# One half of a weight matrix loaded by sixteen DMAs of eight partitions, in a decode-attention kernel

## The chip, the cores and the metric

The kernel runs on one core of a Trainium2 chip. The metric is device time in microseconds (us): the median of three runs of the kernel before is 692.73 us (691.97 to 692.79). Beside these runs there is one profiled execution, which has its own time and from which all durations below are taken.

## The reference, cut to what matters

Two sequences of one token each attend to a cache of 32,768 positions, with 32 query heads on 8 key/value heads of 128 elements. The attention output goes through `wo`, and a small MLP on the same normalized token gates it.

```python
xn = layernorm(A_x)                                  # [2, 1, 512]
q  = (xn @ wq)                                       # 32 heads of 128
o  = softmax(q . k_cache / sqrt(128)) @ v_cache      # caches: [2, 8, 32768, 128] bf16 each
s  = o.reshape(2, 1, 4096) @ wo                      # wo: [4096, 512] bf16
g  = silu(xn + gelu(layernorm(xn) @ w3) @ w4)        # on one token the shifted branch is zero
out = x + s * g
```

The two caches are 268 MB together; every byte of them is read once. `wo` is 4.2 MB.

## The kernel before, in words

The work is cut into 16 units, one for each pair of a sequence and a key/value head (`units`, line 57), and each unit into four chunks of 64 blocks of 128 positions (`NCH` is 4). A chunk of K or of V is one load of 2 MB into one of eight buffers of the pool `slots` ([128 partitions, 8192] bf16; lines 62 and 99). The list `loads` (lines 85 to 92) fixes the order: the first K chunk, `wq` in two loads, the other K chunks of unit 0, `w3`, `w4`, and then K of the next unit and V of this unit in turn. The main loop (lines 376 to 390) walks this list, works on entry i and then issues the load of entry i + 8, into the buffer that entry i has just left. A partition of such a load is one run of 16 KB in memory.

All loads are issued by SyncE (SP) in this order, and SP waits in order too. A load waits for two things: for TensorE to have read the buffer's last content (a semaphore of PE), and for the semaphore that it will raise itself. There are eight of these for DMAs, taken in turn (DMAHW0 to DMAHW7 in the built program), so a DMA waits until the eighth DMA before it has landed.

A K chunk (`k_job`, line 263) is transposed on TensorE, eight blocks at a time (line 250), copied out of PSUM by VectorE or ScalarE in the ratio two to one (lines 253 and 255), and multiplied with the four queries of the unit (line 204). `softmax_front` takes the unit's maximum and the exponentials (line 239). A V chunk (`v_job`, line 275) is multiplied with the probabilities (line 282). `unit_end` (line 296) puts four partial sums together (line 306) and, after every second unit, multiplies four heads with their rows of `wo` (line 316).

`wo` lies in a buffer of its own, `wo_sb` with [128, 32, 512] (line 83). Row h * 128 + p of the matrix goes to partition p, head h. It is loaded in two halves of 16 heads, 2 MB each: the first after the last K chunk of unit 1 (line 388), the second after the first K chunk of unit 2 (line 390). A partition of a half is 16 runs of 1 KB. The first half is needed first by line 316 of unit 1.

Of the kernel before, what the change touches and what calls it, by code (L numbers as in the profile page):

```python
# [22 lines left out]
def kernel(  # L23
# [14 lines left out]
    nc = tc.nc  # L38
# [4 lines left out]
    Hq = HD // Dh  # L43
# [35 lines left out]
    wo_v = A_wo.rearrange("(h p) d -> p h d", p=128)  # L79
# [3 lines left out]
    wo_sb = pers.tile([128, Hq, D], BF16)  # L83
# [11 lines left out]
    def issue(i):  # L95
        if i >= len(loads):
            return
        what = loads[i]
        t = slots.tile([128, UT * Dh], BF16, tag="slot", name=f"slot_{what[0]}")
        if what[0] in ("K", "V"):  # L100
            b, g = units[what[1]]
            c = what[2]
            src = A_k_cache if what[0] == "K" else A_v_cache
            nc.sync.dma_start(
                out=t[:, :],
                in_=src[b, g, c * CH:(c + 1) * CH, :].rearrange("(p t) d -> p (t d)", p=128),
            )
        elif what[0] == "wq":
            k0 = what[1] * 2
            nc.sync.dma_start(  # L110
                out=t[:, 0:2 * HD].rearrange("p (k f) -> p k f", k=2), in_=wq_v[:, k0:k0 + 2, :])
        elif what[0] == "w3":
            nc.sync.dma_start(
                out=t[:, 0:DK * Fdim].rearrange("p (k f) -> p k f", k=DK), in_=w3_v)
        else:
            nc.sync.dma_start(
                out=t[:, 0:FK * D].rearrange("p (f d) -> p f d", f=FK), in_=w4_v)
        tiles[what] = t
# [51 lines left out]
    for j, src in enumerate((xn_bf, ln2_bf)):  # L170
        sv = src[:, :].rearrange("b (p k) -> b k p", k=DK)
        for k in range(DK):
            nc.tensor.transpose(
                out=treg[:, (j * DK + k) * B:(j * DK + k + 1) * B],
                in_=sv[:, k, :], identity=ident[0:B, 0:B])
# [87 lines left out]
    def k_job(n, c):  # L263
        kv = tiles[("K", n, c)][:, :].rearrange("p (t d) -> p t d", d=Dh)
        for blk in range(NB):
            transposed(n, c, blk, kv)
            if n == 0 and c == 0 and blk < KTB - 1:
                if blk == KTB - 2:
                    q_job()
                continue  # L270
            flush(LAG)
            if glue and blk >= 2:
                glue.pop(0)()

    def v_job(n, c):
        vv = tiles[("V", n, c)]
        pr = unit_st[n]["p"]
        for i in range(UT // 16):
            for j in range(4):
                v0 = i * 16 + j * 4  # L280
                u0 = c * UT + v0
                nc.tensor.matmul(  # L282
                    acc[32 * j:32 * j + 16, :],
                    lhsT=pr[:, u0:u0 + 4, :].rearrange("p u h -> p (u h)"),
                    rhs=vv[:, v0 * Dh:(v0 + 4) * Dh],
                    start=(c == 0 and i == 0), stop=(c == NCH - 1 and i == UT // 16 - 1),
                    tile_position=(0, 32 * j),
                )
            if i == 0:
                flush(0)  # L290
        if c == NCH - 1:
            unit_end(n)
# [83 lines left out]
    for i, what in enumerate(loads):  # L376
        if what[0] == "K":
            k_job(what[1], what[2])
        elif what[0] == "V":
            if what[2] == 0:  # L380
                while glue and "p" not in unit_st[what[1]]:
                    glue.pop(0)()
            v_job(what[1], what[2])
        elif what == ("w4",):
            mlp_job()
        issue(i + SLOTS)
        if what == ("K", 1, NCH - 1):
            nc.sync.dma_start(out=wo_sb[:, 0:Hq // 2, :], in_=wo_v[:, 0:Hq // 2, :])
        if what == ("K", 2, 0):
            nc.sync.dma_start(out=wo_sb[:, Hq // 2:Hq, :], in_=wo_v[:, Hq // 2:Hq, :])  # L390
    while glue:
# [37 lines left out]
```

## Time and profile before

| what | value |
|---|---|
| median of three runs | 692.73 us |
| the profiled execution, its own time | 692.67 us |
| its span (first to last instruction) | 690.9 us |
| TensorE busy (matmul) | 557.7 us, 81% of the span |
| VectorE busy, ScalarE busy | 294.1 us and 244.9 us |
| read from memory | 280.50 MB, 406 GB/s over the span |
| mean granted TensorE clock | 0.83 of full speed |

The profile shows one execution. Its second part cuts the span into 40 slices and gives the busy share of each engine in tenths, and below that the mean busy share of the core's 16 DMA engines and what they moved. The third part counts the DMA packets by queue: one is a run of data or a small write that raises a semaphore. The fourth follows the chain of work that ended last back from the end. Views by stretch of time give the same shares for any stretch, the timeline gives single instructions, and the list of waits gives who waited for whom. The trace also keeps, for each DMA, the moments at which the engines that carried it raise its semaphore, and the start, length, size and queue of every packet, but not which engine carried it.

### The profile page before, as it was taken

How to read it: one execution, taken by the hardware profiler on the slowest of the kernel's cores; microseconds unless marked ns; L12 is line 12 of the kernel's file. 1: busy time of each engine (PE TensorE's matmuls, PEld its weight loads, DVE VectorE, ACT ScalarE, POOL GpSimd, SP SyncE). 2: the span in 40 equal slices, each digit the busy share in tenths (PEclk: the TensorE clock that was granted, in tenths of full speed). 3: DMA queues.
4: the chain of work that ended last, by engine and by line, in shares of the span. 5: the costliest groups of instructions: out<-in, count | busy, mean ns of one | idle time of the engine just before them, and what ended most of it. 6: DMA issues, size and time to landing. Idle time of an engine off the chain costs nothing.

```text
span 690.9 us, 20959 instructions
## 1 busy us (share of the span) xinstructions
PE 557.7 (81%) x9662; PEld 468.2 (68%) x9662; DVE 294.1 (43%) x548; ACT 244.9 (35%) x370; POOL 0.9 (0%) x7
## 2 busy tenths in 40 slices
PE   3888998596887988989787869879778896979755
PEld 2885877475876767777676757767676675868633
DVE  4253544232544443534443534344444353445321
ACT  1245343142432433343343424224343342434220
POOL 0000000000000000000000000000000000000000
PEclk9696989678898795868998987799999798799875
DMA  8999999999999999999999999999999999999960
GB/s 360 426 424 427 422 424 401 394 431 421 426 424 423 429 424 424 423 424 426 425 425 426 420 424 428 425 425 424 421 425 428 425 422 426 425 424 426 424 281 18
DMA packets 23231, 281.83 MB, mean 408 GB/s; under 512 B 2148, under 2 KB 6248, under 8 KB 6248
## 3 DMA queue, kind: packets, MB, share of 16 engines
q1 hardware_dynamic: 23144, 280.51, 96.5%
q8 instruction: 75, 1.23, 0.7%
q14 instruction: 12, 0.10, 0.0%
HBM read 280.50 MB, written 0.00 MB: 406 GB/s over the span
## 4 chain that ended last, share of the span: by engine, by line
DMA 63%; PE 30%; ACT 3%; DVE 2%; issue 1%; SPq 0%; ACTq 0%; DVEq 0%
DMA slot_K<-in_A_k_cache_dram 55%; PE tT L250 16%; DMA slot_V<-in_A_v_cache_dram 5%; PE sc L204 4%; PE ot L306 3%; DMA slot_wq<-in_A_wq_dram 2%; PE s_ps L316 2%; ACT ktb L253 2%; PE acc L282 2%; ACT pr L239 1%; PE bc L233 1%; PE ot L304 1%; PE h L363 1%; DVE ktb L255 1%; PE qT L329 1%
## 5 line engine op out<-in xcount | busy, mean ns | idle before, releaser
L250 PE MATMUL tT<-ident,slot_K 128*128 128x128 bf16 x4096 | 349.5, 244 | 80.8 <-DMA slot_K<-in_A_k_cache_dram 78.6
L250 PEld LDWEIGHTS <-slot_K 128*128 128x128 bf16 x4096 | 284.0, 111 | 115.6 <-DMA slot_K<-in_A_k_cache_dram 100.2
L255 DVE COPY ktb<-tT 128x1024 bf16<-128x1024 bf16 x342 | 230.8, 691 | 239.3 <-PE tT L250 238.4
L253 ACT COPY ktb<-tT 128x1024 bf16<-128x1024 bf16 x170 | 172.4, 1014 | 329.1 <-PE tT L250 328.9
L204 PE MATMUL sc<-q_sb,ktb 128*128 128x4 bf16 x4096 | 179.1, 166 | 14.9 <-ACT ktb L253 13.6
L204 PEld LDWEIGHTS <-ktb 128*128 128x128 bf16 x4096 | 155.6, 99 | 43.9 <-ACT ktb L253 26.0
L282 PE MATMUL acc<-slot_V,pr 128*16 128x512 bf16 x1024 | 84.7, 414 | 15.7 <-DMA slot_V<-in_A_v_cache_dram 11.9
L213 DVE TENSOR_REDUCE pm<-sc 128x4 f32<-128x256 f32 x64 | 27.2, 426 | 83.8 <-ACT scS L212 83.8
L239 ACT ACTIVATE pr<-scS,nb 128x256 bf16<-128x256 f32 x64 | 45.0, 853 | 15.8 <-DVE nb L235 15.8
L212 ACT COPY scS<-sc 128x256 f32<-128x256 f32 x64 | 23.8, 372 | 61.9 <-PE sc L204 61.9
L282 PEld LDWEIGHTS <-pr 128*16 128x16 bf16 x1024 | 20.7, 89 | 30.2 <-issue 17.4
L306 PE MATMUL ot<-sel,acs 128*128 128x4 f32 x128 | 23.1, 303 | 0.0
L306 PEld LDWEIGHTS ot<-sel,acs 128*128 128x128 f32 x128 | 22.4, 262 | 0.0
L300 DVE COPY acs<-acc 128x512 f32<-128x512 f32 x16 | 10.9, 683 | 19.1 <-PE ot L306 18.7
L239 ACT ACTIVATION_READ_ACCUMULATOR pr<-scS,nb 128x1 f32 x64 | 16.3, 254 | 0.0
L316 PE MATMUL s_ps<-wo_sb,oT_sb 128*2 128x512 bf16 x32 | 13.2, 559 | 0.5 <-DVE oT_sb L311 0.5
L310 DVE RECIPROCAL rc<-ot 128x4 f32<-128x4 f32 x16 | 2.9, 182 | 23.2 <-PE ot L306 23.2
L233 PE MATMUL bc<-dg,ones_f 4*128 4x4 f32 x32 | 7.5, 301 | 1.3 <-DVE dg L228 1.3
L304 PE MATMUL ot<-S,ones_f 128*128 128x4 f32 x32 | 7.5, 305 | 1.1 <-DVE oT_sb L311 1.1
L329 PE MATMUL qT<-xT,slot_wq 128*128 128x2 bf16 x128 | 3.7, 165 | 5.1 <-DMA slot_wq<-in_A_wq_dram 5.1
L304 PEld LDWEIGHTS ot<-S,ones_f 128*128 128x128 f32 x32 | 6.4, 250 | 2.0 <-DVE oT_sb L311 1.2
L233 PEld LDWEIGHTS bc<-dg,ones_f 4*128 4x128 f32 x32 | 6.1, 237 | 2.1 <-DVE dg L228 1.3
(58 smaller groups left out, 60.2 us busy)
## 6 DMA issues: line engine op xcount, KB each, us to landing
slot_K<-in_A_k_cache_dram SPq DMA_DIRECT2D x64, 2048.0 KB, 31.7
slot_V<-in_A_v_cache_dram SPq DMA_DIRECT2D x64, 2048.0 KB, 35.1
slot_wq<-in_A_wq_dram SPq DMA_DIRECT2D x2, 2048.0 KB, 14.7
wo_sb<-in_A_wo_dram SPq DMA_DIRECT2D x2, 2048.0 KB, 21.0
slot_w<-in_B_w_dram SPq DMA_DIRECT2D x2, 1792.0 KB
x_bf<-in_A_x_dram SPq DMA_DIRECT2D x1, 2.0 KB
out_dram<-out_bf SPq DMA_DIRECT2D x1, 2.0 KB
```

Source lines behind the costliest of these rows:

```text
L204: nc.tensor.matmul(sc[:, u * rep:(u + 1) * rep], lhsT=ktb[:, i, :], rhs=q_sb[:, b, g * rep:(g + 1) * rep], start=True, stop=True,)
L212: nc.scalar.copy(out=st["scS"][:, :, c * UT:(c + 1) * UT], in_=scv)
L213: nc.vector.tensor_reduce(out=st["pm"][:, :, c], in_=scv, axis=AX.X, op=ALU.max)
L233: nc.tensor.matmul(bc[:, :], lhsT=ones_f[0:rep, :], rhs=st["dg"][:, :], start=True, stop=True)
L239: nc.scalar.activation(out=pr[:, :, h], in_=st["scS"][:, h, :], func=ACT.Exp, bias=nb[:, h:h + 1], scale=inv_sqrt_dh, accum_out=S4[:, h:h ...
L250: nc.tensor.transpose(out=tT[:, i, :], in_=kv[:, blk * TB + i, :], identity=ident[:, :])
L253: nc.scalar.copy(out=ktb[:, :, :], in_=tT[:, :, :])
L255: nc.vector.tensor_copy(out=ktb[:, :, :], in_=tT[:, :, :])
L282: nc.tensor.matmul(acc[32 * j:32 * j + 16, :], lhsT=pr[:, u0:u0 + 4, :].rearrange("p u h -> p (u h)"), rhs=vv[:, v0 * Dh:(v0 + 4) * Dh], s ...
L304: nc.tensor.matmul(ot[:, rep:2 * rep], lhsT=ones_f[:, :], rhs=st["S4"][:, :], start=True, stop=True)
L306: nc.tensor.matmul(ot[:, 0:rep], lhsT=acs[:, i * Dh:(i + 1) * Dh], rhs=sel[:, i, :], start=(i == 0), stop=(i == 3))
L316: nc.tensor.matmul(s_ps[:, :], lhsT=oT_sb[:, h, :], rhs=wo_sb[:, h, :], start=(h == 0), stop=(h == Hq - 1))
```

## The change

Only the load of the first half of `wo` is changed. The 128 partitions are taken in 16 groups of eight: group (q, i) has the partitions 32q + i, 32q + i + 4, and so on to 32q + i + 28. Each group is a DMA of [8 partitions, 16 heads, 512], 128 KB in 128 runs of 1 KB. The same bytes go to the same places. The other half, and every other load, is as before.

```diff
         issue(i + SLOTS)
         if what == ("K", 1, NCH - 1):
-            nc.sync.dma_start(out=wo_sb[:, 0:Hq // 2, :], in_=wo_v[:, 0:Hq // 2, :])
+
+            wo_8 = A_wo.rearrange("(h q j i) d -> q i j h d", q=4, j=8, i=4)
+            for q in range(4):
+                for i in range(4):
+                    p0 = 32 * q + i
+                    nc.sync.dma_start(
+                        out=wo_sb[p0:p0 + 29:4, 0:Hq // 2, :], in_=wo_8[q, i, :, 0:Hq // 2, :])
         if what == ("K", 2, 0):
             nc.sync.dma_start(out=wo_sb[:, Hq // 2:Hq, :], in_=wo_v[:, Hq // 2:Hq, :])
```

The built program of the changed kernel has the same instructions in the same order on TensorE, VectorE, ScalarE and GpSimd. On SP the one DMA of line 388 is replaced by sixteen of line 393, between the same two neighbours. Each of the sixteen waits for the next of the eight DMA semaphores, as every DMA here does; the V load behind them waits for DMAHW0, which the ninth of the sixteen raises.

## The prediction

> **What bounds the kernel now.** I read the page's slices first: are the DMA engines ever free?
>
> ```profile
> span 690.9 us, 20959 instructions
> DMA  8999999999999999999999999999999999999960
> GB/s 360 426 424 427 422 424 401 394 431 421 426 424 423 429 424 424 423 424 426 425 425 426 420 424 428 425 425 424 421 425 428 425 422 426 425 424 426 424 281 18
> DMA packets 23231, 281.83 MB, mean 408 GB/s; under 512 B 2148, under 2 KB 6248, under 8 KB 6248
> q8 instruction: 75, 1.23, 0.7%
> DMA 63%; PE 30%; ACT 3%; DVE 2%; issue 1%; SPq 0%; ACTq 0%; DVEq 0%
> ```
>
> They are full from start to near the end, and 63% of the chain that ended last is transfers. The dip to 401 and 394 GB/s is where `wo` is loaded. Then I read the end in stretches of time (columns: stretch, length, busy time of PE, PEld, DVE, ACT, POOL, clock, DMA share, GB/s):
>
> ```profile
> 648.00:652.00 4.00, 1.98 (x41) 1.02 (x37) 0.49 (x2) 1.38 (x2) 0.00 (x0) 1.00 1.03 438
> 660.00:664.00 4.00, 1.70 (x23) 0.79 (x23) 1.76 (x6) 1.24 (x4) 0.00 (x0) 0.86 0.69 291
> 668.00:672.00 4.00, 1.72 (x16) 0.44 (x9) 0.00 (x0) 0.00 (x0) 0.00 (x0) 0.79 0.48 205
> 676.00:680.00 4.00, 2.37 (x19) 0.97 (x18) 0.00 (x0) 0.00 (x0) 0.00 (x0) 0.50 0.01 4
> ```
>
> At 668 us half of the sixteen engines have nothing left. The semaphore events of the last V load say the same: eight engines end at 661.4 to 667.0 us, the other eight at 675.0 to 677.6. In the first K load all were within 1.2 us. What parts them is instruction loads: 75 packets of 16 KB on q8, of about 1.1 us. Followed by their start times, they take eight engines in turn, and each visit sets an engine back 1.5 us. So **there are eight late engines, which fetch instructions, and eight early ones**, and the end (677.6, and 13.3 us of last V product, sums and output) hangs on the late eight alone.
>
> Last, SP's timeline where `wo` is issued:
>
> ```profile
> 89.20 0.33 SPq L104 DMA_DIRECT2D slot_K<-in_A_k_cache_dram  x1
> 89.58 0.43 SPq L388 DMA_DIRECT2D wo_sb<-in_A_wo_dram  x1
> 91.11 27.58 SPq L104 DMA_DIRECT2D slot_V<-in_A_v_cache_dram  x1
> 118.78 0.73 SPq L104 DMA_DIRECT2D slot_K<-in_A_k_cache_dram  x1
> ```
>
> The V load behind `wo` was issued for 27.58 us: its descriptors went in only when `wo` began to drain. This costs nothing, because the engines had earlier loads to do. The events give, for that place: the K load issued at 89.20 lands on the early engines at 114.6 to 116.0 and on the late ones at 116.3 to 119.0; `wo` 5.9 us later on each (120.5 to 121.9, and 122.2 to 124.9); V 4.9 us after that.
>
> **The change, part by part.**
>
> *Which engines carry the sixteen DMAs.* The packets under 512 B are semaphore writes: 134 loads over 128 partitions at 16 each are 2144, and 4 are left for the two DMAs of two partitions (x_bf and the output), two each. So a DMA of two partitions runs on two engines, and I take it that one of eight runs on eight. [...]
>
> *Bytes per engine.* A half of `wo` costs an engine 5.9 us (114.62 to 120.53 on the first, 119.02 to 124.85 on the last). On eight engines it is twice that, 11.8 us, or 0.74 us for each of the sixteen. So eight engines get +5.9 us and eight get -5.9 us, and all hangs on whether the loaded eight are the late ones.
>
> *Issue and waits.* Fifteen more issues at 0.33 to 0.43 us are 5 to 6.5 us of SP, which is no cost in itself: SP sat 27.58 us in this place. But each waits for the eighth DMA before it, and that binds here as elsewhere:
>
> ```profile
> SPq L104 <- DMA slot_K<-in_A_k_cache_dram: 55.2, 31, 3.8
> ```
>
> DMAs 1 to 7 of the sixteen wait for loads landing up to 113.9 and go out in time. The eighth waits for the K load that lands at 119.0. The ninth waits for the first of the sixteen, and the V load behind them for the ninth. Until then nothing is queued for the other eight engines: they run dry from 116 to 119 us on.
>
> *If the early eight carry the load.* The ninth lands at 116.0 + 9 x 0.74 = 122.7. SP also needs nine issues (eighth to sixteenth) from 119.0 on at a step of 0.40 to 0.47 us (x_bf to K at the start, and the issues of 136 to 138 us), so V is issued at 122.7 to 123.25. From issue to first packet the first K load took 0.97 us on its first engine and 1.83 on its last, so the late engines start V at 123.7 to 125.1, where before the last of them started at 124.85. They skip 5.9 us of `wo` and stand idle for nearly all of it: -1.2 to +0.2, and I take **-0.6 us**, nearer the first rows because a step of 0.40 is what a short row of issues showed when nothing was queued. The early eight end at 661.4 to 667.0 plus 5.9, at most 672.9, still ahead.
>
> *The second half and the next V.* V issued behind the second half was held 14.76 us (120.08) without an engine going dry. Now the loaded eight reach that half at 116.0 + 11.8 + 2 x 4.9 = 137.6, which releases that V; the others need it at 124.4 + 2 x 4.9 + 5.9 = 140.1. About 1.5 us of cover is left after the 0.97; if it is gone, each us late is a us on the end.
>
> *Consumers.* Line 316 reads the first half from 143.9 us on. It would land at 127.8 or 130.8 instead of 124.9, still 13 us early. No engine but SP has another instruction. At 134.9 TensorE waits for a K load, which moves by some us; it is made up, since TensorE is 81% busy and does not set the end.
>
> [...]
>
> **The rivals.**
>
> A, the forecast: the loaded eight are the early ones. 692.67 - 0.6 = **692.1 us**, own range 691.4 to 693.0. The profiled time stands 0.06 below the median, so nothing is added.
>
> B, slower: the fetching engines are among the loaded eight. Then the last of them does all sixteen from 119.0 to 130.8 instead of 124.9; V waits for the ninth only until 125.7 and is there in time, so there is no further gap. 677.6 + 5.9, and 692.67 + 5.9 = **698.6** (697.5 to 699.3; less, 695.6, if only a fetching engine that ends 2.6 us earlier is loaded). It decides as soon as one of the three engines that end last is loaded. [...]
>
> C, nothing is shifted: the DMAs are spread over sixteen engines, by shape or by partition. Bytes per engine stay. The sixteenth is issued at 122.3 to 122.8, the queue is just short, and V starts at about 125.0 to 125.3 instead of 124.9: **692.9**.
>
> D, as A but no gap, if the waits hold less than I read: the early eight end last, at 672.9, 4.7 us before 677.6: **688.0**. The list of waits speaks against it.
>
> **How the numbers follow.** A 0.52, B 0.36, C 0.07, D 0.05. What a measurement of this kernel can tell from no change is about 0.2%, 1.4 us. Of A, 0.14 may end beyond it on the faster side (a gap shorter than reckoned), 0.02 on the slower. Faster: 0.14 + 0.05 = 0.19. Slower: 0.36 + 0.02 + 0.02 of C = 0.40. Same: 0.41. The range goes from A's lower end to B's upper, 691.2 to 699.2, because B alone is more than 2 in 10.
>
> **What would show it.** Packets: with eight engines each, 16 x 8 - 16 = 112 more (23343, and 2260 under 512 B); with sixteen, 240 more. Semaphore events: the sixteen land about 0.74 us apart. A stretch of some 4 to 5 us with a DMA share near 0.5 around 119 to 124. At the end, A has the early engines finish at 667 to 673 us and the late ones still at 677, so the stretch at half share shrinks to a few us; B has both some 6 us later (early ones idle from 116 to 126.7, late ones at 683), and the stretch keeps its length. I am wrong at the root if the sixteen run on all engines, or if the V load behind them is issued before 121 us.

## The result, and the profile after

The changed kernel takes **697.69 us** (median of four runs, 697.12 to 698.46) against 692.42 of the kernel before on the same chip (691.97 to 692.79): ratio 1.0077, 95% interval 1.006 to 1.0095. It is 5.3 us slower. The profiled execution took 698.25 us.

The page after, the lines that answer to those shown of before:

```profile
span 696.5 us, 20977 instructions
DMA  8999998899999999999999999999999999999970
GB/s 361 426 422 429 421 425 331 309 407 420 428 423 425 426 423 424 424 426 424 423 426 423 424 428 423 426 423 427 421 425 427 422 427 423 424 425 423 426 322 22
DMA packets 23343, 281.83 MB, mean 405 GB/s; under 512 B 2260, under 2 KB 6360, under 8 KB 6360
q8 instruction: 75, 1.23, 0.7%
DMA 68%; PE 26%; ACT 2%; DVE 1%; SPq 1%; issue 1%; ACTq 0%; DVEq 0%
```

The packets have grown by 112: each of the sixteen runs on eight engines. Slices 7 and 8 (104 to 139 us) fell from 401 and 394 to 331 and 309 GB/s. Slice 9 fell from 431 to 407, since the second half of `wo` now lands in it (144.6 to 146.5 us). All others up to the end are within 8 GB/s of what they were, so the time was lost in this one place and not made up. SP's timeline there:

```profile
88.52 0.33 SPq L104 DMA_DIRECT2D slot_K<-in_A_k_cache_dram  x1
88.90 36.70 SPq L393 DMA_DIRECT2D wo_sb<-in_A_wo_dram  x16
125.71 0.40 SPq L104 DMA_DIRECT2D slot_V<-in_A_v_cache_dram  x1
126.21 0.37 SPq L104 DMA_DIRECT2D slot_K<-in_A_k_cache_dram  x1
```

In the kernel before, the V load was handed to its queue from 91.1 us on; now SP comes to it at 125.71. Stretches of time around that, and at the end (stretch, length, busy PE, PEld, DVE, ACT, POOL, clock, DMA share, GB/s):

```profile
118.00:120.00 2.00, 0.81 (x12) 0.82 (x13) 0.11 (x1) 0.00 (x0) 0.00 (x0) 0.91 0.42 149
124.00:126.00 2.00, 1.60 (x42) 1.56 (x40) 1.34 (x2) 1.03 (x2) 0.00 (x0) 1.00 0.47 138
128.00:130.00 2.00, 0.00 (x0) 0.00 (x0) 0.00 (x0) 0.00 (x0) 0.00 (x0) 0.97 1.11 245
...
668.00:672.00 4.00, 1.51 (x16) 0.54 (x17) 0.00 (x0) 2.43 (x8) 0.00 (x0) 0.50 0.81 336
676.00:680.00 4.00, 1.74 (x16) 0.54 (x16) 0.00 (x0) 0.00 (x0) 0.00 (x0) 0.50 0.47 201
680.00:684.00 4.00, 0.99 (x16) 0.31 (x15) 0.00 (x0) 0.00 (x0) 0.00 (x0) 0.50 0.14 57
```

At 118 to 126 us about half of the engines or fewer have work (a share of 0.42 to 0.52). At 128 us all are busy and still move only 245 GB/s, which is something else than idleness. At the end the stretch at half share lies some 6 us later than before (205 GB/s at 668 to 672 us then; 201 at 676 to 680 now).

The semaphore events give the same by load. The K load ahead of the sixteen lands at 114.6 to 119.1 us, as before. The first of the sixteen lands on six of its engines at 115.4 to 116.3 and on two at 118.7 and 118.8: **six of the loaded engines are early ones and two are late ones**. The sixteenth lands at 128.7 to 131.0. The V load behind lands at 133.8 to 135.7 on all sixteen (125.5 to 129.8 before): the lead that the early engines had is used up, and the last engine is 5.9 us later. The last V load of the kernel ends at 669.5 to 675.8 on the early engines and at 680.1 to 683.1 on the late ones, 5.5 us later than before at its end.

### The profile page after: what moved, and what is told of

Its sections match the earlier page's. It is cut to its first block, busy times and chain, and to the rows that moved or that the text cites. A ratio compares the mean times of both kernels' runs of the same rounds, so it can differ in the third digit from the quotient of the medians.

```text
span 696.5 us, 20977 instructions
## 1 busy us (share of the span) xinstructions
PE 551.3 (79%) x9662; PEld 463.0 (66%) x9662; DVE 293.8 (42%) x548; ACT 244.7 (35%) x370; POOL 0.9 (0%) x7
## 4 chain that ended last, share of the span: by engine, by line
DMA 68%; PE 26%; ACT 2%; DVE 1%; SPq 1%; issue 1%; ACTq 0%; DVEq 0%
DMA slot_K<-in_A_k_cache_dram 60%; PE tT L250 14%; DMA slot_V<-in_A_v_cache_dram 5%; PE sc L204 3%; DMA slot_wq<-in_A_wq_dram 2%; PE ot L306 2%; PE s_ps L316 2%; ACT ktb L253 1%; PE acc L282 1%; SPq L393 1%; ACT pr L239 1%; PE h L363 1%; PE bc L233 1%; PE ot L304 1%; PE qT L329 1%
## 5 line engine op out<-in xcount | busy, mean ns | idle before, releaser
L306 PE MATMUL ot<-sel,acs 128*128 128x4 f32 x128 | 20.6, 284 | 0.0
L306 PEld LDWEIGHTS ot<-sel,acs 128*128 128x128 f32 x128 | 19.8, 236 | 0.0
L316 PE MATMUL s_ps<-wo_sb,oT_sb 128*2 128x512 bf16 x32 | 11.4, 494 | 0.5 <-DVE oT_sb L311 0.5
L329 PEld LDWEIGHTS <-slot_wq 128*128 128x128 bf16 x128 | 3.5, 104 | 5.5 <-DMA slot_wq<-in_A_wq_dram 5.5
```

The source lines that it names most:

```text
L306: nc.tensor.matmul(ot[:, 0:rep], lhsT=acs[:, i * Dh:(i + 1) * Dh], rhs=sel[:, i, :], start=(i == 0), stop=(i == 3))
L316: nc.tensor.matmul(s_ps[:, :], lhsT=oT_sb[:, h, :], rhs=wo_sb[:, h, :], start=(h == 0), stop=(h == Hq - 1))
L329: nc.tensor.matmul(qT_ps[:, h * B:(h + 1) * B], lhsT=w[:, (k % 2) * HD + h * Dh:(k % 2) * HD + (h + 1) * Dh], rhs=xT[:, k, :], start=(k == ...
```

## The experiments

Three explanations were kept apart. *Shift*: two of the eight loaded engines are late ones, and carry twice their share of half a `wo`. *Gap*: the V load is held behind the sixteen, and the engines run dry. *Write side*, which came up after the second run: the time depends on which partitions the eight engines write.

| run | us, median | ratio to before, 95% interval |
|---|---|---|
| the change | 697.69 | 1.0060 to 1.0095 |
| e1 sixteen DMAs, one head each, 128 partitions | 694.54 | 1.0024 to 1.0049 |
| e2 the sixteen, one behind each of the first 16 loads | 707.04 | 1.0200 to 1.0229 |
| e3 the sixteen carry one head, one DMA the rest | 700.75 | 1.0105 to 1.0136 |
| e4 small probes in the kernel before | 692.77 | one run |
| e5 as e2, into partitions 0 to 63 only | 695.86 | 1.0044 to 1.0068 |
| e6 as e2, upper partitions first | 706.84 | 1.0182 to 1.0215 |
| e7 small probes in the changed kernel | 698.60 | one run |
| e8 half of the last V load over 125 partitions | 695.75 | 1.0041 to 1.0070 |
| e9 eight consecutive partitions each | 705.01 | 1.0159 to 1.0205 |
| e10 the change, into partitions 0 to 63 only | 696.42 | 1.0045 to 1.0075 |
| e11 the sixteen on ScalarE's queue | 708.40 | 1.0212 to 1.0246 |
| e12 as e11, into partitions 0 to 63 only | 707.65 | 1.0211 to 1.0242 |
| e13 one cache load cut into DMAs of 25, 25, 5, 5, 4 and 64 partitions | 702.01 | 1.0129 to 1.0159 |
| e14 two such loads | 718.91 | 1.0368 to 1.0399 |
| e15 the sixteen on GpSimd's queue, partitions 0 to 63 | 701.00 | 1.0107 to 1.0140 |

### The gap by itself: e1 and e3

e1 keeps sixteen issues in the same place but cuts by head, so that each runs on all sixteen engines and nothing is shifted.

```diff
-            for q in range(4):
...
+            for h in range(Hq // 2):
+                nc.sync.dma_start(out=wo_sb[:, h:h + 1, :], in_=wo_v[:, h:h + 1, :])
```

> The first half of wo is again sixteen DMAs of 128 KB in the same place, but each takes one head over all 128 partitions, so each should run on sixteen engines (134 + 15 DMAs over 128 partitions: 2388 packets under 512 B). Theory 1 (the 5.5 us come from late, instruction-fetching engines among the eight that carry the sixteen DMAs): bytes per engine are as before, so the time is that of before within 0.5 us. Theory 2 (they come from the queue running dry, because the V load is held behind sixteen issues that wait for one another): the issues and waits are the same, so some of the loss stays, 1 to 4 us, by how long an issue takes (0.4 or 0.7 us).

Its timeline shows the same hold:

```profile
86.09 0.33 SPq L104 DMA_DIRECT2D slot_K<-in_A_k_cache_dram  x1
86.47 36.63 SPq L389 DMA_DIRECT2D wo_sb<-in_A_wo_dram  x16
123.20 0.38 SPq L104 DMA_DIRECT2D slot_V<-in_A_v_cache_dram  x1
```

V is issued at 123.20, lands everywhere at 130.3 to 131.2, 1.4 us later than before on the last engine, and the last V load of the kernel ends at 679.0, again 1.4 us later. So sixteen issues in this place cost about 2 us with no byte moved to another engine.

e3 lets the sixteen DMAs of eight partitions carry one head only (8 KB), and sends the other fifteen heads over 128 partitions behind them.

```diff
-                        out=wo_sb[p0:p0 + 29:4, 0:Hq // 2, :], in_=wo_8[q, i, :, 0:Hq // 2, :])
+                        out=wo_sb[p0:p0 + 29:4, 0:1, :], in_=wo_8[q, i8, :, 0:1, :])
+            nc.sync.dma_start(out=wo_sb[:, 1:Hq // 2, :], in_=wo_v[:, 1:Hq // 2, :])
```

> Sixteen DMAs of eight partitions in the same place, but of one head each (8 KB), and the other 15 heads by one DMA over 128 partitions behind them. The shift between engines is 1/16 of the change's (0.4 us), the waits and issues stay. Theory 1: within 1 us of before. Theory 2: every engine runs dry until the big DMA is issued, behind the K load that lands at 119 us and nine more issues: 3 to 8 us slower than before.

Nearly nothing is shifted here, and it is slower than the change itself. The sixteen take 0.62 to 0.74 us each to issue though they are tiny; the large one goes out at 124.69 on dry engines and lands at 132.1 to 132.8, where the half of `wo` landed by 124.9 before. The whole half now starts after the gap, in place of filling it: 7.9 us there, 7.9 at the end (685.5).

### Which engines are late: e4 and e7

Small DMAs of n partitions, n from 1 to 15, between the cache loads of the middle. Which completion moments are added from n to n + 1 tells where engine n stands.

```diff
+    PROBES = {80 + 3 * j: j + 1 for j in range(15)}
...
+        if i in PROBES:
+            n_p = PROBES[i]
+            nc.sync.dma_start(out=probe[0:n_p, n_p - 1, :], in_=A_wo[0:n_p, 0:32])
```

> The kernel before with fifteen small DMAs added, of 1 to 15 partitions and 64 B each, one behind every third load from 300 us on (nothing reads them). If a DMA of n partitions runs on the n lowest engines, each of them completes on n engines, and these are nested, so the times at which they complete beside those of the load ahead tell engine by engine which are late. Theory 1: the first eight hold two late engines (as the 118.7 us among 115.4 to 116.3 of the first of the sixteen suggests) and six early ones. Were the late eight all outside the first eight, theory 1 falls.

Completion moments, us, of some of the probes (sorted):

```
n=5   509.8 509.8 511.2 511.5 514.1
n=6   524.5 524.5 525.9 526.2 528.8 536.5
n=7   539.2 539.2 540.6 540.9 543.5 551.1 551.3
n=8   553.9 554.0 554.0 555.3 556.3 558.2 565.8 565.9
n=15  656.9 657.0 657.0 657.0 658.5 659.4 662.2 | 670.3 670.4 670.5 670.5 670.5 672.0 672.1 672.9
```

The set grows by one engine at a time. The sixth and seventh member (engines 5 and 6) come some 8 us behind the fifth; the eighth is early again, the ninth early, and the next six late. So, counted from 0 in the order in which they join, **engines 5, 6 and 9 to 14 are the late ones, and 0 to 4, 7, 8 and 15 the early ones** (the last by what is left, since the loads have eight of each); a DMA of eight partitions runs on 0 to 7 and so on two late engines. The trace has no engine numbers: these count the order of joining in e4 and nothing else.

e7 puts seven such probes into the changed kernel.

> The changed kernel with seven small DMAs of 5 to 8 partitions of 64 bytes among the cache loads of the middle, whose completion times show where engines 5 and 6 (loaded and late) stand beside the late ones that got no half of wo. Theory of shifted bytes: engines 5 and 6 land 3 to 6 us behind the other late ones, and end last. Theory of the gap: all sixteen started V within 2 us of each other, so 5 and 6 stand within 2 us of the other late ones. Time 697.7 us by both, within 0.8.

The last probe of seven partitions lands at 670.7, 671.0, 672.4, 672.7, 675.2, 683.6 and 683.6; the V load just ahead of it at 668.8 to 675.0 on the early engines and at 679.7, 679.8, 680.0, 681.3, 681.4, 681.5, 683.4 and 683.4 on the late ones. So engines 5 and 6 end last, 1.9 us behind the late engines that got nothing of the first half. And those six, which skip 5.9 us of `wo`, still end at 681.5 where the last late engine ended at 677.6 before: **without a byte more, late engines lose about 4 us**. That is the gap, together with whatever the writes of the other eight cost them.

### The write side: e2, e5, e6 and e10

e2 was meant as the shift without a gap: one of the sixteen behind each of the first sixteen loads, with time to spare.

```diff
+        if i < 16:
+            q, r = i // 4, i % 4
+            p0 = 32 * q + r
...
+            nc.sync.dma_start(
+                out=wo_sb[p0:p0 + 29:4, 0:Hq // 2, :], in_=wo_8[q, r, :, 0:Hq // 2, :])
```

> The same sixteen DMAs of eight partitions, but one behind each of the sixteen loads issued from 22 to 90 us, so that no engine runs dry; the same engines carry the same bytes. Theory 1: the late engines among the eight still do 5.9 us more, so 3.3 to 6 us slower than before (a late engine that ends 2.6 us before the last costs the less). Theory 2: no gap, no loss; the late engines outside the eight even gain, so 0 to 4 us faster than before.

Both theories missed it by far, and the stretches show how:

```profile
65.00:90.00 25.00, 22.44 (x475) 18.28 (x473) 13.79 (x23) 11.46 (x17) 0.00 (x0) 0.99 1.01 420
90.00:115.00 25.00, 19.52 (x269) 17.60 (x270) 8.92 (x18) 8.08 (x14) 0.00 (x0) 0.66 1.02 327
115.00:140.00 25.00, 11.19 (x190) 9.06 (x190) 4.55 (x8) 3.78 (x5) 0.00 (x0) 0.67 1.01 334
```

From 90 us on the engines are as busy as ever and move a fifth less. That begins when the ninth of the sixteen lands (92.6 us), the first that goes to partitions 64 to 127. On the first of the engines that carry nothing extra a load takes 5.8 to 6.4 us there, and 4.9 before. e6 turns the order of the groups around (`q, r = 3 - i // 4, i % 4`), so that the upper partitions come first.

> The interleaved run with the four groups in the opposite order: partitions 96 to 127 and 64 to 95 first, then the lower ones. Theory of the write side: the stretch of some 325 GB/s at a full DMA share moves from 90-140 us to about 45-90 us, and is over once the lower groups' turn comes; the time stays near 707 us. Theory of shifted bytes alone: 707 us with the slow stretch wherever the lead of the engines is used up, 90-140 us again. Theory of the gap: no slow stretch, 692 us, which the interleaved run has already spoken against.

```profile
40.00:65.00 25.00, 20.43 (x340) 16.03 (x336) 11.34 (x26) 12.52 (x19) 0.00 (x0) 0.86 1.01 361
65.00:90.00 25.00, 17.50 (x320) 13.94 (x320) 8.66 (x14) 7.59 (x11) 0.00 (x0) 0.78 1.03 344
115.00:140.00 25.00, 20.40 (x344) 16.77 (x342) 8.93 (x15) 7.19 (x9) 0.00 (x0) 0.76 1.00 405
```

The slow stretch moves to the front with the upper groups (e2 had 421 GB/s at 40 to 65 us), and is over when the lower ones come. e5 keeps engines, bytes and places in the order, and writes the lower half only (`p0 = 32 * (q % 2) + r`). It leaves zeros in the upper half, so it serves for its time alone, as do e10, e12 and e15.

> Sixteen DMAs of eight partitions as in the interleaved run, one behind each of the first sixteen loads, but all of them write partitions 0 to 63 (the rows of the two upper groups overwrite those of the two lower ones), and partitions 64 to 127 of the first half of wo hold zeros written by GpSimd: that part of wo's first half is replaced. Bytes read, engines and number of descriptors are those of the interleaved run, and the queue never runs dry. Theory of shifted bytes (eight engines carry 5.9 us more, two of them late ones): the last of the late ones ends 5 to 6 us later, 697 to 698.5 us, and the window of 90 to 140 us moves over 400 GB/s. Theory of the gap alone: at most 0 against before, 692.5 us or less. Theory of the write side (engines 0 to 7 writing the upper partitions get in the way of the engines that write there otherwise): the loss of 14.5 us of the interleaved run is gone down to the 5 us of the shift. If the write side has nothing to do with it: about 707 us again.

```profile
90.00:115.00 25.00, 21.95 (x313) 18.70 (x301) 10.48 (x21) 8.58 (x16) 0.00 (x0) 0.66 1.02 422
...
130.00:134.00 4.00, 3.80 (x91) 3.43 (x88) 2.46 (x4) 1.90 (x2) 0.00 (x0) 1.00 0.85 322
134.00:138.00 4.00, 1.11 (x20) 0.47 (x20) 1.19 (x3) 0.49 (x2) 0.00 (x0) 0.83 0.49 191
```

422 GB/s where e2 had 327, and 11.2 us less: the loss is bound to the partitions that are written. The upper partitions are not slow as such: a load over all 128 writes them too, at 420 to 425 GB/s. Why eight engines that write there lose so much, the runs do not show.

e5 is also a measure of the **shift**, though not a clean one. SP was held for 17.88 us at 121 us, and the eight unloaded engines ran dry at 130 to 138 us (share 0.85, then 0.49), so that they lost time too; by the events of the loads the loaded eight went on almost without a break. It costs 3.8 us, of the 5 to 6 expected. e10 puts the same, lower half only, in the place of the change:

```diff
-                    p0 = 32 * q + i
+                    p0 = 32 * (q % 2) + i
```

> The changed kernel with all sixteen DMAs writing partitions 0 to 63 (the two upper groups' rows overwrite those of the two lower ones) and zeros from GpSimd in partitions 64 to 127 of wo's first half: that part is replaced. It measures what the writes into the upper partitions cost at this place, where little else flows while the sixteen run. Write side as dear as in the interleaved run: 3 us or more below 697.7. Write side only dear beside full traffic: 0 to 1.5 us below, since only the last eight DMAs write there and run on a nearly dry queue. Theories of the gap and of shifted bytes: 697.7 us.

696.42 us, 1.3 below the change (the intervals overlap; in the profiles V lands at 133.9 in place of 135.7, and the end comes at 681.1 in place of 683.1). The same stretch as above shows where:

```profile
128.00:130.00 2.00, 0.00 (x0) 0.00 (x0) 0.00 (x0) 0.00 (x0) 0.00 (x0) 0.50 1.06 434
```

434 GB/s in place of 245, both at a full share: in the change the last of the sixteen, in the upper half, meet the V load that has just started. So the write side has 1 to 2 us of the change's 5.3; before V is issued, about half of the engines or fewer have work (the share of 0.42 to 0.52 above).

e10 also shows the shift in the place of the change. On the last of its loaded engines the sixteen land at 118.65 to 129.0, each 0.67 to 0.79 us behind the one before, so this engine never stood idle; V lands there 4.9 us later, at 133.9, where the last engine of the kernel before had it at 129.8. These 4.1 us owe nothing to a dry queue. The eight unloaded engines, which did run dry, land V at 132.4 to 133.2.

### What the issue costs: e9

Eight consecutive partitions in place of eight that lie four apart, all else as in the change.

```diff
+            for g in range(16):
+                nc.sync.dma_start(
+                    out=wo_sb[8 * g:8 * g + 8, 0:Hq // 2, :], in_=wo_v[8 * g:8 * g + 8, 0:Hq // 2, :])
```

> The changed kernel with eight consecutive partitions in each of the sixteen DMAs in place of eight that lie four apart; same bytes, same engines, same place. If the 0.68 us that SP spends on each issue comes from the stride, the issues take 0.33 to 0.43 us, the V load behind them is issued at 122.7 to 123.3 in place of 125.7, the engines that got no half of wo land it at 131 to 132 in place of 134 and the loaded ones at 134 to 135.7: theory of the gap 694.5 to 695.5 us, theory of shifted bytes (5.9 us on the loaded late engines whatever the issues do) 697 to 698 us. If the 0.68 us belongs to eight partitions as such, nothing moves: 697.7 us by both.

The issues themselves fell to 0.27 to 0.33 us for most of them, so the 0.68 us does come from the stride. But V got no earlier:

```profile
86.91 38.57 SPq L390 DMA_DIRECT2D wo_sb<-in_A_wo_dram  x16
126.12 0.35 SPq L104 DMA_DIRECT2D slot_V<-in_A_v_cache_dram  x1
```

The sixteen now take an engine about 1 us each in the lower half (0.8 to 1.3) and up to 1.8 in the upper, where the change's took 0.65 to 0.7 with a full queue, and every issue from the eleventh on waits for one of them. V lands at 137.0 to 140.9, and the time is 7.3 us above the change: what the issues saved, eight engines that write into eight neighbouring partitions lost several times over.

### Other queues: e11, e12 and e15

The sixteen were given to ScalarE (`nc.scalar.dma_start`), so that V need not wait; e12 also writes the lower half only.

> The changed kernel with the sixteen DMAs issued by ScalarE in place of SyncE, so that the V load is issued at once as in the kernel before (about 91 us) and the sixteen run beside the cache loads. Theory of the gap: with the wait behind sixteen issues gone, the loss is gone, 692 to 693 us. Theory of shifted bytes: the late loaded engines keep their extra, 694.5 to 698 us. Theory of the write side: eight of the sixteen now write the upper partitions beside full traffic, which cost the interleaved run some 11 us beyond the run that wrote the lower half only: 700 to 708 us.

> The sixteen DMAs on ScalarE's queue as in the run before this one, but all into partitions 0 to 63, with zeros in the upper partitions of wo's first half: that part is replaced. No gap on SyncE and no writes into the upper partitions: what is left is the shift of bytes to the first eight engines, two of them late. Theory of shifted bytes: engines 5 and 6 end 2 to 5.9 us later, 694.5 to 698 us. Theory of the gap: 692 to 693 us. Theory of the write side: whatever the shift costs, and less than the run before this one by 5 us or more.

These two say nothing on the shift, because ScalarE itself stood still (e11, ScalarE's timeline; the bracket is the idle time of the engine before):

```profile
88.35 44.03 ACTq L393 DMA_DIRECT2D wo_sb<-in_A_wo_dram  x16
132.42 0.37 ACT L212 COPY scS<-sc 128x256 f32<-128x256 f32 x1 [43.08 <-DMA wo_sb<-in_A_wo_dram]
```

The first three of the sixteen landed at 105.5, 115.4 and 121.8 us on their first engine, 9.9 and 6.4 us apart, where a load of SP's queue landed every 4.9 us. The later ones waited for the eighth before them, ScalarE waited with them, and no buffer came free. On GpSimd's queue nothing stands behind the sixteen:

> The changed kernel with the sixteen DMAs issued by GpSimd, which has no other work here and may wait, all into partitions 0 to 63, with zeros in the upper partitions of wo's first half: that part is replaced. SyncE issues the V load at once, nothing waits behind the sixteen, and ScalarE isn't blocked as it was on its own queue. Theory of shifted bytes: engines 5 and 6 carry 16 rows more in place of 8, 4 to 5.9 us, and end last: 695.5 to 698 us. Theory of the gap: 692 to 693 us. If GpSimd's DMAs are slow to start they land late, at a use that lies past 140 us, and the time could be 700 us and more.

```profile
q0 software_dynamic: 1280, 2.11, 0.9%
20.00:40.00 20.00, 17.17 (x394) 16.93 (x395) 6.67 (x12) 5.71 (x7) 3.20 (x6) 1.00 1.02 362
```

(The first line is from the page's list of queues, the second from the stretches.) GpSimd has nothing else to do here and issued them from 8.5 to 43 us. The packets are 80 per DMA, where ScalarE's queue had 136, eight of them semaphore writes: here they are 32 of 4 KB, 32 of 16 bytes and sixteen semaphore writes. Which engines carried the data, the trace does not say, but the cache loads behind show no shift (the one issued at 74.5 lands at 103.8 to 108.8, over 5 us as in the kernel before). The rate stayed at 348 to 362 GB/s for the first 60 us, at a full share from 20 us on. So it does not test the shift, and its loss has the look of the write side.

### Rows moved off the late engines: e8, e13 and e14

If the late engines set the end, a kernel that takes rows from them should beat both. e8 sends half of the last V load over 125 partitions; e13 cuts the 101st load of the list into DMAs of 25, 25, 5, 5, 4 and 64 partitions, and e14 the 71st too. All three were meant to give engines 0 to 4 more and the late ones less, 2.45 us of a late engine for each load that is cut. That DMAs of 25 and of 125 partitions stay on engines 0 to 4 was the author's estimate: the probes of e4 end at 15 partitions, and no view of e8, e13 or e14 shows it.

```diff
+            cut = (0, 25, 50, 55, 60, 64, 128) if i == 100 else (0, 128)
+            for lo, hi in zip(cut, cut[1:]):
+                nc.sync.dma_start(out=t[lo:hi, :], in_=ap[lo:hi, :])
```

> [...] The late engines carry half of the last load, 2.5 us less each; the five early ones get some 8 us more from a lead of 8 to 14 us. Theory of shifted bytes: the end moves by -2.5 to 0 us, 690 to 692.5 us. Theory of the gap: 692.5 us, nothing changed. Theory of the write side: the five engines write the upper partitions in the way of the others in the last 10 us, so 692.5 to 697 us.

> [...] Theory of shifted bytes (the last late engine sets the end): 2.45 us less at the end, 689.8 to 690.8 us. Theory of the gap: 692.5 us. [...]

> As the run before this one, with two such loads (the 71st and the 101st). Late engines move eight rows fewer, 4.9 us; engine 4 has 16 more rows, 9.8 us, and stood 8 us ahead of the early late ones. Theory of shifted bytes: late engines end at 670 to 672.7 and engines 0 to 4 at 672 to 677, so the end hangs on engine 4: 689 to 692 us. Theory of the gap: 692.5 us.

All lost: e8 3.7 us, e13 9.9, e14 26.8. Around the cut load of e13:

```profile
490.00:500.00 10.00, 7.98 (x144) 7.21 (x144) 3.48 (x6) 3.41 (x4) 0.00 (x0) 0.83 1.00 420
500.00:510.00 10.00, 8.38 (x137) 7.86 (x129) 6.20 (x14) 4.69 (x10) 0.00 (x0) 0.83 0.96 315
510.00:520.00 10.00, 5.80 (x94) 4.95 (x94) 1.81 (x3) 1.88 (x3) 0.00 (x0) 0.66 0.92 211
520.00:530.00 10.00, 4.65 (x89) 3.02 (x86) 2.46 (x4) 1.90 (x3) 0.00 (x0) 0.80 1.00 213
```

Half the bytes at a nearly full share, for 20 us. Whatever DMAs over few partitions cost here, it is far more than the 2.45 us that the late ones were to be spared; it looks like the write side again, but no run tells it apart from the odd split of the rows. No version here beats the kernel before.

## Why the prediction was wrong

**Where it held.** Transfers bound the kernel, and the end hangs on the late engines. A DMA of eight partitions runs on eight engines (112 packets more, as written). The eighth issue waits for the K load (issued at 119.16, K landed at 119.1). That eight engines are late and eight early was told rightly. No run names the engines of the sixteen: that all go to the same eight, on which the +5.9 and -5.9 us rest, was the author's estimate. What the change shows is one pattern of landing: each of the first seven lands on six engines, 0.66 to 0.69 us behind the one before it, and on two more 2.3 us behind the last of these six; and the DMA share is 0.42 to 0.52 from 118 to 126 us.

**The step that failed: when the other engines start V.** The prediction had V issued at 122.7 to 123.25 and started at 123.7 to 125.1, against 124.85 before, and took -0.6 us. Two terms were too small. The issue step was set at 0.40 to 0.47 us; it is 0.72 for partitions that lie four apart, so nine of them end at 125.7. And a load on a dry queue was given its first packet's delay, 0.97 to 1.83 us, and then the 4.9 us of a flowing load, 5.9 to 6.7 together; it took 7.1 to 8.0 us from issue to landing in e1 and 7.0 to 7.7 on the unloaded engines of e10. In the change itself it is 8.1 to 8.6, of which by e10 about 1 us is the write side, a term that the sum did not have. The row for it was in the trace before: the first K load was issued at 1.14 and landed at 7.95 to 9.15 us, 6.8 to 8.0 later. Together, the unloaded engines land V at up to 134.3 in place of 129.8: +4.5 us where -0.6 stood (+3.4 in e10), and e7 finds six late ones about 4 us later at the end. The stretch near half share, put at 4 to 5 us, was some 8 us long (118 to 126). So by these rows forecast A was wrong in its own case too: with only early engines loaded the kernel would still have been slower, though no run has that case by itself.

**The choice of engines.** "The loaded eight are the early ones" against "the fetching engines are among the loaded eight" was the author's estimate, 0.52 against 0.36: no row of the trace before names an engine. It is neither whole set: engines 5 and 6 are late, the other six early. The end needs one late engine only, so rival B came nearest, and its chain came true: sixteen done at 131.0 (130.8 in the prediction), V landed at 135.7, the time 697.69 (698.6). B's price supposed that one of the three engines that end last is loaded; whether 5 or 6 is one of these in the kernel before, no trace tells, but in e7 the two end last. It also had the last loaded engine begin at 119.0; the first of the sixteen lands on the two late ones at 118.7 and 118.8, so they began at about 118.1, and the engine that ended the K load at 119.1 was not loaded. And the agreement is partly luck in the sizes. In the lower half a DMA takes 0.69 us of a loaded engine (fifteen steps from 118.65 to 129.0 in e10), not 0.74, and the upper half adds 2 us that the prediction did not know of. The range held the result only because it was drawn up to B, which had 0.36; the forecast itself pointed the other way. (Its bounds, 691.2 and 699.2, are not quite the 691.4 and 699.3 that A and B are given.)

**How the 5.3 us divide.** Gap and shift do not add: they are two ways to the same moment, V's landing on the last engine. e10 has both and no upper half: the gap brings the unloaded engines to 133.2 and the shift the loaded ones to 133.9, and the time is +3.9, near the +3.8 of e5. The upper half then adds 1 to 2 us on the loaded ones. After that moment nothing changes; it and the end move together in every run with the sixteen in this place:

| run | V behind the first half lands, last engine | last V load ends | us |
|---|---|---|---|
| before | 129.8 | 677.6 | 692.42 |
| e1 | 131.2 | 679.0 | 694.54 |
| e10 | 133.9 | 681.1 | 696.42 |
| the change | 135.7 | 683.1 | 697.69 |
| e3 | 137.7 | 685.5 | 700.75 |
| e9 | 140.9 | 688.6 | 705.01 |

**The other steps.** The 1.5 us of cover at the second half was not used up: V there is issued at 127.2 and held 13.42 us, and no stretch at 140 to 162 us falls under a full share (1.06 at 142 to 152). B's sign for the end, both groups some 6 us later and the stretch at half share as long as before, came true in part: the late engines end 5.1 to 5.5 us later and the early ones 8.1 to 8.8, so the stretch is some 3 us shorter. Rivals C and D fell with the 112 packets and the late V.

**What stays open.** No whole run has the shift by itself: e10 shows it on one engine, beside a gap on others, e5 has another place and a dry stretch on the unloaded engines, and the queues of e11, e12 and e15 brought losses of their own. The write side's part of the time is small beside the spread of the runs (the intervals of e10 and the change overlap), so it rests on the 245 against 434 GB/s and on V's landing. What the write side waits for, no view of the trace shows. And why the stride in the partitions raises the issue from 0.27 to 0.68 us was not followed up.

## What to carry to other kernels

Where a queue is kept full by long loads, price a change by the moment at which the next long load lands on the slowest engine; here a run of small DMAs ahead of it cost its issues (0.72 us each in the change), its waits for earlier semaphores, and a restart on dry engines (7 to 8 us from issue to landing of a load that takes 4.9 in the flow, e1 and e10). The DMAs over eight partitions did not only sit on eight engines: which partitions these wrote mattered too (327 GB/s in e2, 422 in e5), and in e2, e13 and the change a fifth to a half of the rate went at a full busy share. So look at GB/s beside the share, not at the share alone.

## What the runs showed of the hardware

- In the kernel before, eight of the sixteen engines land the last V load at 675.0 to 677.6 us and the other eight at 661.4 to 667.0; together the late ones are 115 us behind the first landing, by estimate 1.5 us for each of the 75 instruction packets on q8. By the order in which the probes of e4 join, they are 5, 6 and 9 to 14.
- DMA issues on SP that are not held take 0.33 to 0.48 us over 128 partitions (before, the change) and 0.27 to 0.33 us over eight neighbouring ones (e9); over eight that lie four apart they take 0.62 to 0.83 us, whether they carry 8 KB (e3) or 128 KB (the change).
- Sixteen DMAs of eight partitions, 128 KB each, cost 11 us more with eight of them in partitions 64 to 127 than with all in 0 to 63 beside full traffic (e2 less e5, 707.04 and 695.86), and 1 to 2 us more beside a DMA share of 0.42 to 0.52 (the change less e10, 697.69 and 696.42).
- Eight neighbouring partitions of the lower half are written at about 1 us for 128 KB (e9), eight that are spread over 32 at 0.65 to 0.7 (the change).
- A chain of sixteen DMA issues on ScalarE held that engine for 44 us (e11), each waiting for the eighth DMA of the kernel before it to land.
